# Nineteen relative features per head in a linear attention layer: the twentieth exponential as a preset one

## The chip, the cores and the metric

The kernel runs on one core of one Trainium2 chip. The metric is the device time of one execution in microseconds, the median over repeated runs; lower is better. The profiler records one execution and gives a span from the first to the last instruction of the program.

In the text PE is the tensor engine (matrix products), DVE the vector engine, ACT the scalar engine (activations), POOL the GpSimd engine, and SP the engine whose queue issues nearly all transfers.

## What is computed

A block with layernorm, a linear attention with softmax features, a residual, and a second layernorm with a SiLU feed-forward part and a residual. There are 2048 tokens of 640 values and 32 heads of 20.

```python
qkv = (layernorm(x) @ wqkv)              # q, k, v: 32 heads of 20
pq = einsum("bhsd,hdf->bhsf", q, w_phi)  # 20 features per head
pk = einsum("bhsd,hdf->bhsf", k, w_phi)
phi_q = concat([softmax(pq), softmax(-pq)])   # 40 per head
phi_k = concat([softmax(pk), softmax(-pk)])
kv = einsum("bhsf,bhsd->bhfd", phi_k, v)
z = phi_k.sum(over tokens)
o = einsum(phi_q, kv) / (einsum(phi_q, z) + 1e-6)
h = x + o @ wo
out = h + silu(layernorm(h) @ w1) @ w2        # w1: 640 x 1728
```

A softmax does not change when one number is subtracted from all its arguments. That is the fact which the change uses.

## The kernel before

The 2048 tokens are 16 tiles of 128, and the token index t runs over these. The program has these stages, which overlap:

- **Prologue.** PE is kept running with dummy products (`warm0` to `warm19`) while the key weights arrive in five pieces (`WK0` to `WK4`). Each piece is transposed (`wk`, evicted by `wke`), multiplied by the block diagonal of `w_phi` (`fk`, 640 columns in two banks) and evicted by ACT into `Wfk` (`fk0e` to `fk4e`). So the feature projection is folded into the key weights, and a key projection gives features at once. The same is done for the queries (`fq0` to `fq5`, into `Wfq`), from weights that a transposing transfer brings.
- **Normalisation** of a tile: `st` (moments, DVE), `rs` (inverse deviation, ACT or POOL), `xn` (the normalised tile, DVE or POOL), `xt` (its transpose, by PE for the first four tiles, by a transposing transfer on SP's queue for the others).
- **Keys and values**, per tile: `K` (ten matmuls of 320 columns), `ex` (two exponentials on ACT, of the features and of their negatives, into one of four key buffers `EK`), `su` (sums over each run of 20, DVE), `rk` (inverse of the sums, ACT), `sc` (scaling in place, DVE), `V` and `ve` (values, into one of eight buffers `VP`), `kv` (eleven matmuls that add the tile to the state of all heads). Each head has 40 features, each group of three heads one stationary operand of 128 columns.
- **Queries**, per tile: `Q` (ten matmuls; 33 heads' worth, one of them a head of zeros), `qe` (exponentials into `EQ`, all tiles in one buffer), `qs`, `ql`/`qi`/`qr` (sums, ratio, scaling of one half), `qt` (transpose by transfer).
- **Attention**, per tile: `D` (eleven matmuls), `E` (division, two halves), `ot` (transpose by transfer), `G` (output projection, two groups of five matmuls of 320 columns), `ga` (residual), `ls`, `lr`, `hn`, `ht` (second normalisation and its transpose).
- **Feed-forward**, for units of two or four tiles: `u` (up projection, up to 512 columns), `s` (SiLU), `d` (down projection), `oa` (residual), `out` (store).

The order of all these steps is written out by hand in one list, `ORDER`, of some 900 names. The program walks it and emits each step; each engine then runs its own instructions in that order and waits by semaphores. `su2` is the sum of tile 2, `G10` the first group of tile 1's output projection, `u0.12` the piece of unit 0 that begins at block 12. A dictionary `ON` says for some steps which engine they run on. The projections share three pairs of PSUM banks in turn (`ps_pair`), so a projection also waits until the one three places back has been evicted.

Of the kernel before, what the change touches and what calls it, by code (L numbers as in the profile page):

```python
# [18 lines left out]
warm0 warm1 warm2 warm3 warm4 warm5 warm6 warm7 warm8 warm9 warm10 warm11 warm12 warm13 warm14 pad0 mask  # L19
ones0 ones3 X0 st0 WK2 WK3 phi_a WK0 wk2 warm15 warm16 warm17 warm18 warm19 rs0 X1 phi_b WK1 WK4 wk3  # L20
wke2 wke3 wk0 wke0 xn0 xt0 X2 mask0 st1 wk1 wke1 fk3 wk4 x0 WV0 fk1 rs1 X4 fk3e fk1e fk2 xn1 own fk0 WV3
fk2e wke4 st2 V0.0 ones5 fk0e fk4 wph1 st3 xt1 K0s fk4e WV2 rs2 K0.2 x1 WV4 K0.1 st4 K0.0 xn2 K0.4 rs3
K0.3 ones1 ex0 K1 st6 V0.3 WV1 V0.2 rs4 su0 X8 xt2 V1 V0.1 ex1 xn3 xn4 x2 ve1 xt3 x3 wq2 V0.4 ve0 st5
rs5 K2 rk0 st9 st7 K3 wq3 su1 ex2 ex3 sc0 V2 ve2 wph0 rk1 st8 xn5 phq V3 xt4 rs9 st12 ve3 rs6 wq1 rs7
load10 kv0 ones2 xn6 K4 ex4 V4 sc1 fq3 ones7 ve4 rs8 kv1 xn7 xt5 wq0 xn8 xn9 fq3e xt6 V5 su2 xt7 wq5 rk2
su3 ve5 rk3 wq4 K5 sc2 ex5 fq0 K6 kv2 sc3 st11 kv3 fq0e xt8 fq2 ex6 st10 su4 fq2e su5 rs11 V6 ve6 st13
fq1 K7 st14 V7 fq1e rk4 xt9 rs10 xn10 ex7 zeros ve7 su6 rs13 V8 sc4 ve8 fq4 V9 ones4 load0 xt10 load5
fq5 fq4e rk5 rk6 su7 ve9 K8 sc5 xn11 kv4 load7 fq5e rs14 K9 rk7 sc6 rs12 ex8 kv5 Q0 sc7 ex9 qe0 xn14
ones6 K10 su8 xt11 xn12 kv6 load2 xn13 su9 st15 rs15 kv7 qs0 xt12 xn15 Q1 rk8 V10 ex10 sc8 qe1 ve10
load3 ql0 K11 V11 xt13 rk9 ex11 qs1 su10 qi0 ve11 ql1 eqp rk10 kv8 K12 V12 ex12 qi1 sc9 ve12 load4 su11  # L30
sc10 kv9 K13 rk11 V13 kv10 qr0 xt14 K14 su12 ex13 rk12 sc11 su13 ve13 xt15 ex14 rk13 K15 kv11 V14 Q2
ex15 qr1 qt0 load1 qt1 mask1 ve14 load6 V15 sc12 Q3 su14 kv12 su15 sc13 rk14 rk15 kv13 sc14 qe2 kv14
ve15 sc15 qs2 kv15 bd1 load9 qe3 Q5 Q7 halves ql2 qe5 qe7 bd0 qi2 qr2 qs3 D0 E00 E01 D1 E10 ql3 Q4 E11
qe4 qt2 Q9 qi3 Q6 qe9 qs5 ql5 D2 qi5 Q8 ot0 ot1 qr3 G00 G01 qs4 qe6 E20 qr5 E21 ql4 G10 ga01 Q10 qe8 qi4
ga00 qe10 ga10 qt3 Q11 D3 qr4 qt5 ls0 G11 qe11 Q14 Q12 E30 Q13 lr0 ot2 qe14 ga11 qe12 qe13 ls1 qt4 E31
hn0 lr1 ot3 Q15 G20 hn1 ht1 qs6 G21 qe15 qs7 ht0 D5 G30 load8 pad1 ga20 qr6 ga21 ga30 G31 load11 E50 E51
D4 u0.12 E40 u0.4 u0.0 s0.0 s0.12 ga31 ls3 u0.6 E41 ot5 qs8 u0.L u0.2 ls2 qr7 s0.6 u0.8 qt6 lr2 s0.4 ot4
u0.10 D6 s0.L G50 s0.10 G40 lt0 qt7 lr3 s0.8 E60 G51 E61 s0.2 d10 ot6 ga40 hn2 ga50 ga51 ls5 hn3 lr5 G41
d00 D7 d01 ga41 ls4 G60 lr4 hn5 G61 E70 ht2 ht3 hn4 oa10 ht5 d11 qr8 oa00 ht4 ga61 u2.2 u2.0 ga60 qt8
E71 ot7 s2.0 oa01 qs9 u2.L qs13 s2.2 qr9 oa11 qs11 u2.6 D8 u2.10 E80 ls6 qt9 u2.7 u2.3 s2.L u2.11 s2.10  # L40
s2.6 qr13 E81 u2.9 s2.9 qr11 u2.5 qs12 s2.7 qs10 s2.3 u2.1 D9 G70 s2.5 E90 qr10 u2.12 s2.11 E91 ot8 G71
u2.4 lr6 ga71 ga70 qt11 out0 lt2 s2.1 qt10 u2.8 out1 hn6 s2.4 qr12 ls7 G80 s2.8 ga80 ot9 G81 D11 s2.12
E110 d30 ht6 qt13 E111 d20 D10 ga81 lr7 G90 E100 oa30 oa20 E101 ot10 G91 hn7 ga91 d31 ot11 ga90 ls8 qs15
lr8 d21 qt12 oa31 d50 G100 ls9 G101 hn8 out3 d40 d51 ht8 lr9 hn9 oa21 ga101 G110 out2 ga100 ga110 oa50
oa40 G111 qs14 d41 oa51 D12 ls10 ht7 E120 ht9 u6.1 u6.0 oa41 ga111 u6.12 u6.8 D13 s6.0 s6.1 qr14 s6.8
E121 s6.12 u6.11 ot12 u6.2 u6.3 qr15 lr10 s6.11 u6.L s6.2 E130 ls11 out4 E131 u6.9 qt15 s6.3 G120 ot13
s6.L u6.6 lt6 s6.6 lr11 u6.7 u6.10 hn10 u6.5 out5 s6.7 hn11 s6.9 u6.4 qt14 G121 ga120 ga121 s6.5 ht11
G130 D14 G131 E140 ga131 s6.10 s6.4 d60 ls12 oa60 d61 d70 ht10 lr12 E141 d91 ga130 ls13 oa61 hn12 oa70
D15 lr13 d90 ht12 ot14 d71 hn13 ht13 out6 G140 oa71 oa90 u10.L oa91 ga140 out9 E150 u10.0 u10.1 out7
E151 u10.6 G141 u10.9 s10.L s10.0 s10.6 u10.8 ga141 d80 u10.7 s10.1 u10.3 u10.11 ot15 s10.3 u10.5 u10.12  # L50
oa80 s10.9 s10.8 s10.11 u10.2 u10.4 ls14 s10.7 s10.5 u10.10 s10.12 s10.4 G150 G151 lt10 lr14 d81 s10.10
s10.2 d110 hn14 oa81 ht14 out8 d111 ga150 d120 ga151 ls15 d101 lr15 d100 hn15 oa100 oa110 ht15 oa101
d121 oa111 out10 oa120 out11 u14.L u14.4 u14.0 oa121 s14.0 s14.L u14.8 u14.6 s14.6 u14.2 d131 u14.12
u14.10 s14.2 s14.4 d130 lt14 oa130 oa131 s14.12 s14.10 out13 s14.8 out12 d140 d141 oa140 d150 oa141
out14 d151 oa150 out150 d152 oa151 out151 oa152 out152
# [4 lines left out]
def kernel(  # L60
# [20 lines left out]
    DH = 20  # L81
    HF = 2 * DH
# [19 lines left out]
    proj_ctx = ctx.enter_context(ExitStack())  # L102
    proj = proj_ctx.enter_context(tc.tile_pool(name="proj", bufs=1, side="right"))
# [33 lines left out]
    NE = 4  # L137
# [56 lines left out]
    NV = 8  # L194
    VP = [persist.tile([P, H, HV], BF16, name=f"VP{i}") for i in range(NV)]

    EK = [persist.tile([P, FCH * (NCH - 1) + P], BF16, name=f"EK{i}") for i in range(NE)]
# [27 lines left out]
    Wfk = proj.tile([P, C, D], BF16, name="Wfk")  # L225
    Wfq = proj.tile([P, C, D + DH], BF16, name="Wfq")

    def ones(i):
        nc.gpsimd.memset(VP[i][:, :, DH:HV], 1.0)
        if i < NE:  # L230
            nc.gpsimd.memset(EK[i][:, H * HF :], 0.0)

# [17 lines left out]

    add("zeros", lambda: nc.gpsimd.memset(Wfq[:, 0, D : D + DH], 0.0))

# [70 lines left out]

    def folded(eng, Wf, key, ce):
        eng(Wf[:, ce, 0:D].rearrange("p (g n) -> p g n", g=2), ps_of.pop((key, ce))[:, :, 0:HD])  # L325
# [11 lines left out]
    LW = D - (NQ - 1) * QW  # L337
    WPQ = early.tile([P, NQ, DH], BF16, name="WPQ")
    own_q = early.tile([P, 2, BH], BF16, name="own_q")
    phi_q = early.tile([P, NQ, QW], BF16, name="phi_q")  # L340
# [49 lines left out]
    def width(r):  # L390
        return min(QW, D - QW * r)
# [13 lines left out]
    def folded_block(eng, r):  # L405
        eng(Wfq[:, :, QW * r : QW * r + width(r)], ps_of.pop(("fq", r)))
# [86 lines left out]
    def project(t, W, key):  # L493

        ps = ps_of[key, t] = ps_pair()
        for g in range(2):
            for c in range(C):
                nc.tensor.matmul(  # L498
                    ps[:, g, 0:HD],
                    XnT[:, c, t * P : (t + 1) * P],  # L500
                    W[:, c, g * HD : (g + 1) * HD],
# [19 lines left out]
    def first_key_chunk(c):  # L521

        first_keys.append(c)
        for g in range(2):
            nc.tensor.matmul(  # L525
                ps_of["K", 0][:, g, 0:HD], XnT[:, c, 0:P], Wfk[:, c, g * HD : (g + 1) * HD],
# [5 lines left out]
    def project_queries(t, g, ps):  # L532
        a, b = (DH * h for h in Q_PARTS[g])
        for c in range(C):
            e = b if c == 0 else min(b, D)
# [12 lines left out]
    def key_exps(t):  # L548
        ek[t] = EK[t % NE]
        p4 = ps_of.pop(("K", t))[:, :, 0:HD].rearrange("p g (h f) -> p g h f", f=DH)  # L550
# [416 lines left out]
```

## Time and profile before

| what | value |
|---|---|
| median of three runs | 234.9 us (234.73 to 234.98) |
| profiled execution, span | 232.8 us |
| granted clock of PE | 1.000 |
| busy, PE / DVE / ACT / POOL | 228.0 / 164.0 / 107.4 / 62.6 us |
| moved by DMA | 26.79 MB |

The span counts from the first to the last instruction of the program; the device time of a run holds what lies around it too. Of the profiled execution no other time is given than its span. In the rows of the profile a line such as "L498 PE MATMUL" is a group of instructions of one source line; the first numbers after the bar are its busy time in us and the mean of one in ns, the numbers behind the second bar are the idle time ahead of it and what ended it. In the chain of work that ended last and in the timeline, the first column is the start in us and the second the length; an "xN" is the number of instructions merged. A row of transfers ends with the median time from issue to landing.

### The profile page before, as it was taken

The page shows a single profiled execution, that of the slowest core. Times are in us where ns is not written, and L with a number is a line of the kernel's source. Part 1 is how long each engine was busy: PE and PEld are TensorE (multiplying, and loading weights), DVE is VectorE, ACT ScalarE, POOL GpSimd, SP SyncE. Part 2 cuts the span into 40 slices and gives each one's busy share as a digit, 9 for nine tenths or more (in the row PEclk, how much of TensorE's full clock was granted, in tenths as well). Part 3 has the DMA queues.
Part 4 walks back from the last instruction along what each step waited for, and adds up shares of the span by engine and source line. Part 5 has one row for each costly group of instructions (what it writes and reads, how often), then busy time and mean ns, then how long its engine had stood idle before and what let it go on. Part 6 is the DMA issues. An engine that isn't in the chain of part 4 may idle for free.

```text
span 232.8 us, 5040 instructions
## 1 busy us (share of the span) xinstructions
PE 228.0 (98%) x1977; PEld 160.5 (69%) x1984; DVE 164.0 (70%) x340; ACT 107.4 (46%) x241; POOL 62.6 (27%) x99
## 2 busy tenths in 40 slices
PE   7999999999999999999999999999999999999995
PEld 5777777777777778877545777655677455778874
DVE  4989999999999899998999794891472330404031
ACT  2899999998879884410344000064200235001400
POOL 7589896995001120211010111110020010100000
PEclk9999999999999999999999999999999999999999
DMA  6995379698836766696236956137213301011011
GB/s 169 336 291 103 87 119 217 217 145 188 220 115 114 159 116 136 124 121 146 56 66 154 120 114 158 30 80 172 55 28 85 99 0 28 31 28 56 8 56 56
DMA packets 67213, 26.79 MB, mean 115 GB/s; under 512 B 60151, under 2 KB 66167, under 8 KB 67063
## 3 DMA queue, kind: packets, MB, share of 16 engines
q1 hardware_dynamic: 66535, 26.47, 49.9%
q8 instruction: 15, 0.25, 0.5%
q10 hardware_dynamic: 656, 0.03, 0.2%
q14 instruction: 7, 0.06, 0.1%
HBM read 9.64 MB, written 2.62 MB: 53 GB/s over the span
## 4 chain that ended last, share of the span: by engine, by line
PE 95%; DMA 2%; SPq 1%; issue 1%; ACT 1%; DVE 0%
PE banks L890 24%; PE banks L850 24%; PE banks L498 18%; PE banks L536 9%; PE banks L767 9%; PE banks L589 2%; PE banks L734 2%; PE banks L893 2%; DMA Wk<-in_A_wqkv_dram 2%; PE banks L861 1%; PE banks L525 1%; PE banks L400 1%; ACT Wfk L325 1%; SPq L166 1%; PE banks L510 0%
## 5 line engine op out<-in xcount | busy, mean ns | idle before, releaser
L870 ACT ACTIVATE shT<-banks 128x512 bf16<-128x512 f32 (+1 forms) x53 | 28.5, 591 | 84.2 <-PE banks L850 84.2
L890 PE MATMUL banks<-w_sb,shT 128*128 128x320 bf16 (+2 forms) x429 | 61.3, 295 | 0.0
L850 PE MATMUL banks<-HnT,w_sb 128*128 128x512 bf16 (+1 forms) x318 | 58.4, 335 | 0.4
L890 PEld LDWEIGHTS <-shT 128*128 128x128 bf16 x429 | 41.1, 98 | 15.2
L850 PEld LDWEIGHTS <-w_sb 128*128 128x128 bf16 x325 | 31.2, 98 | 22.1
L899 DVE TENSOR_TENSOR o_t<-banks,X 128x320 bf16<-128x320 f32 (+2 forms) x33 | 14.9, 474 | 39.6 <-PE banks L893 26.7
L443 POOL TENSOR_SCALAR rs<-mv 128x1 f32<-128x1 f32 x21 | 5.8, 276 | 113.2 <-DVE mv L435 113.2
L498 PEld LDWEIGHTS <-XnT 128*128 128x128 bf16 x300 | 28.5, 98 | 10.3
L450 POOL TENSOR_SCALAR xn<-X,mv,rs 128x640 bf16<-128x640 bf16 x12 | 31.3, 2615 | 4.1 <-ACT rs L441 2.1
L434 DVE BATCH_NORM_STATS2 st<-X 128x6 f32<-128x320 bf16 x64 | 27.9, 477 | 4.3 <-DMA X<-in_A_x_dram 4.0
L767 PE MATMUL banks<-wo_sb,OT 128*128 128x320 bf16 x160 | 24.8, 299 | 0.0
L662 DVE TENSOR_REDUCE Sq<-EQ 128x66 f32<-128x1320 bf16 x16 | 23.9, 1512 | 0.0
L774 DVE TENSOR_TENSOR X<-banks,X 128x320 bf16<-128x320 f32 x32 | 14.7, 483 | 13.0 <-PE banks L767 12.9
L658 ACT ACTIVATE EQ<-banks 128x360 bf16<-128x360 f32 (+2 forms) x52 | 22.0, 514 | 3.2 <-PE banks L536 3.1
L557 DVE TENSOR_REDUCE Sk<-EK 128x64 f32<-128x1280 bf16 x16 | 23.3, 1468 | 0.2 <-ACT EK L553 0.2
L536 PE MATMUL banks<-Wfq,XnT 128*128 128x360 bf16 (+2 forms) x160 | 23.3, 299 | 0.0
L498 PE MATMUL banks<-Wv,XnT 128*128 128x320 bf16 x150 | 22.5, 299 | 0.0
L498 PE MATMUL banks<-Wfk,XnT 128*128 128x320 bf16 x150 | 22.5, 299 | 0.0
L553 ACT ACTIVATE EK<-banks 128x640 bf16<-128x640 f32 x32 | 20.5, 698 | 1.4 <-PE banks L498 1.2
L767 PEld LDWEIGHTS <-OT 128*128 128x128 bf16 x160 | 15.2, 98 | 6.5
L536 PEld LDWEIGHTS <-XnT 128*128 128x128 bf16 x160 | 15.2, 97 | 6.2
L747 DVE TENSOR_TENSOR O<-banks,Rd 128x360 bf16<-128x360 f32 (+1 forms) x32 | 15.7, 491 | 1.1
(76 smaller groups left out, 203.0 us busy)
## 6 DMA issues: line engine op xcount, KB each, us to landing
out_dram<-o_t SPq DMA_DIRECT2D x15, 160.0 KB, 2.0
w_sb<-in_B_w_dram SPq DMA_DIRECT2D x5, 432.0 KB, 4.8
w_sb<-in_B_w_dram SPq DMA_DIRECT2D x3, 480.0 KB, 4.1
X<-in_A_x_dram SPq DMA_DIRECT2D x1, 1280.0 KB, 8.4
Wk<-in_A_wqkv_dram SPq DMA_DIRECT2D x5, 160.0 KB, 3.8
Wv<-in_A_wqkv_dram SPq DMA_DIRECT2D x5, 160.0 KB, 4.9
wo_sb<-in_A_wo_dram SPq DMA_DIRECT2D x1, 800.0 KB, 6.5
X<-in_A_x_dram SPq DMA_DIRECT2D x1, 640.0 KB, 5.9
```

The lines of the kernel that those rows point to most:

```text
L434: nc.vector.bn_stats(st[:, i, :], X[:, t, i * HD : (i + 1) * HD])
L450: eng.tensor_scalar(out=xn_[t][:], in0=X[:, t, :], scalar1=mv_.pop(t)[:, 0:1], scalar2=rs_.pop(t)[:], op0=ALU.subtract, op1=ALU.mult,)
L498: nc.tensor.matmul(ps[:, g, 0:HD], XnT[:, c, t * P : (t + 1) * P], W[:, c, g * HD : (g + 1) * HD], start=(c == 0), stop=(c == C - 1),)
L536: nc.tensor.matmul(ps[:, 0 : e - a], XnT[:, c, t * P : (t + 1) * P], Wfq[:, c, a:e], start=(c == 0), stop=(c == C - 1),)
L553: nc.scalar.activation(E5[:, :, :, b, :], p4, AF.Exp, scale=sign)
L557: nc.vector.tensor_reduce(sk[t][:], ek[t][:, 0 : H * HF].rearrange("p (q f) -> p q f", f=DH), axis=AX.X, op=ALU.add)
L658: nc.scalar.activation(features(t, a, b)[:, :, :, i], p4, AF.Exp, scale=sign)
L662: nc.vector.tensor_reduce(sq[t][:], EQ[0][:, t, :, 0:FCH].rearrange("p c (q f) -> p c q f", f=DH), axis=AX.X, op=ALU.add)
L767: nc.tensor.matmul(ps[:, 0:HD], ot[t][:, c, :], wo_sb[:, c, g * HD : (g + 1) * HD], start=(c == 0), stop=(c == C - 1),)
L850: nc.tensor.matmul(ps[:, at : at + n], w1_sb[:, c, fc * P : fc * P + P], HnT[u][:, c, 0:n], start=(c == 0), stop=(c == C - 1),)
L870: nc.scalar.activation(shT[u][:, f0 * n : f1 * n], ps_of.pop(("u", u, f0))[:, 0 : (f1 - f0) * n], AF.Silu)
L890: nc.tensor.matmul(ps[:, 0 : b - a], shT[u][:, at : at + P], w2_sb[:, fc, a:b], start=(fc == 0), stop=False,)
```

## The change

Instead of 20 features per head the projections give 19: the folded matrix holds the columns of `w_phi` minus its last column. The twentieth feature is then always zero and its exponential always one. Its slot in the key buffers and in `EQ` is written by POOL: a memset of four-byte words, each two bfloat16 ones, covers slots 18 and 19 of each run, and the exponential then writes slots 0 to 18. As `sc` scales a key buffer in place, the slots are written again each time the buffer is used again (`ref5` to `ref15`, each after `kv` of the tile that used the buffer last); the first five are written within `ones0` to `ones4`, those of `EQ` by `eqr0` (tiles 0 to 3) and `eqr1`.

Key projections go from 320 to 304 columns a matmul. Query projections go from 660 and four times 640 columns a tile to 627 and four times 608. There are five key buffers for four and seven value buffers for eight; they move to a pool that is closed with the projection's tiles. The sums and scalings still run over 20 slots. The order of all steps is new.

```diff
+    DR = DH - 1
+    HR = H // 2 * DR
+    DP = H * DR
...
+    keys = proj_ctx.enter_context(tc.tile_pool(name="keys", bufs=1, side="right"))
...
-    NE = 4
+    NE = 5
...
-    NV = 8
-    VP = [persist.tile([P, H, HV], BF16, name=f"VP{i}") for i in range(NV)]
-    EK = [persist.tile([P, FCH * (NCH - 1) + P], BF16, name=f"EK{i}") for i in range(NE)]
+    NV = 7
+    VP = [keys.tile([P, H, HV], BF16, name=f"VP{i}") for i in range(NV)]
+    EK = [keys.tile([P, FCH * (NCH - 1) + P], BF16, name=f"EK{i}") for i in range(NE)]
...
-    Wfk = proj.tile([P, C, D], BF16, name="Wfk")
-    Wfq = proj.tile([P, C, D + DH], BF16, name="Wfq")
+    Wfk = proj.tile([P, C, DP], BF16, name="Wfk")
+    Wfq = proj.tile([P, C, DP + DR], BF16, name="Wfq")
+
+    TWO_ONES = 1.0 + 0x3F80 / 2**23
+
+    def reference_slots(i):
+        w = EK[i][:, 0 : H * HF].bitcast(F32).rearrange("p (q f) -> p q f", f=DH // 2)
+        nc.gpsimd.memset(w[:, :, DH // 2 - 1 : DH // 2], TWO_ONES)
 
     def ones(i):
         nc.gpsimd.memset(VP[i][:, :, DH:HV], 1.0)
         if i < NE:
             nc.gpsimd.memset(EK[i][:, H * HF :], 0.0)
+            reference_slots(i)
...
+    WPD = early.tile([P, C, DR], BF16, name="WPD")
...
+        if b == 0:
+            nc.vector.tensor_tensor(
+                WPD[:], WPH[:, :, 0:DR], WPH[:, :, DR:DH].to_broadcast([P, C, DR]), op=ALU.subtract
+            )
...
+    def eq_references(a, b):
+        w = EQ[0][:].rearrange("p t c f -> p (t c f)").bitcast(F32).rearrange("p (t c f) -> p (t c) f", c=NCH, f=P // 2)
+        r = w[:, a * NCH : b * NCH, 0 : FCH // 2].rearrange("p c (q f) -> p c q f", f=DH // 2)
+        nc.gpsimd.memset(r[:, :, :, DH // 2 - 1 : DH // 2], TWO_ONES)
+
+    add("eqr0", lambda: eq_references(0, 4))
+    add("eqr1", lambda: eq_references(4, T))
...
-        p4 = ps_of.pop(("K", t))[:, :, 0:HD].rearrange("p g (h f) -> p g h f", f=DH)
+        p4 = ps_of.pop(("K", t))[:, :, 0:HR].rearrange("p g (h f) -> p g h f", f=DR)
...
-            nc.scalar.activation(E5[:, :, :, b, :], p4, AF.Exp, scale=sign)
+            nc.scalar.activation(E5[:, :, :, b, 0:DR], p4, AF.Exp, scale=sign)
...
-            add(f"K{t}", lambda t=t: project(t, Wfk, "K"))
+            add(f"K{t}", lambda t=t: project(t, Wfk, "K", HR))
...
+        if t >= NE:
+            add(f"ref{t}", lambda t=t: reference_slots(t % NE))
```

The same replacement of 20 by 19 is made in the folds (two more subtractions on POOL within `phq`), in `project_queries` and in `query_exps`. Of the two orders, these are the stretches of which the text speaks; first the prologue, then the middle of the key stage, then the first output projections, then the first up projection:

```diff
-wke2 wke3 wk0 wke0 xn0 xt0 X2 mask0 st1 wk1 wke1 fk3 wk4 x0 WV0 fk1 rs1 X4 fk3e fk1e fk2 xn1 own fk0 WV3
+WK2 WK3 WK0 st0 warm15 wk2 warm16 own wk3 wke3 warm17 ones1 wk0 phi_b warm18 warm19 X1 rs0 WK1 pad0 wke2
+WK4 wke0 X2 st1 fk3 fk3e wk1 rs1 wk4 xn0 wke1 fk2 fk2e ones3 ones0 xt0 fk1 WV0 fk1e X4 wke4 mask xn1 fk0
...
-ones6 K10 su8 xt11 xn12 kv6 load2 xn13 su9 st15 rs15 kv7 qs0 xt12 xn15 Q1 rk8 V10 ex10 sc8 qe1 ve10
+xt11 rk6 kv5 K10 ex9 V11 rk7 xn12 su8 rk8 sc6 kv6 qe0 su9 ref10 xn14 ref11 xt12 rs15 ex10 sc7 Q1 K11
+xt14 rk9 ve11 xn13 V10 qe1 ex11 kv7 sc8 kv8 su10 K12 ve10 ref12 xn15 rk10 load4 eqr1 qs0 sc9 ex12 su11
...
-qe4 qt2 Q9 qi3 Q6 qe9 qs5 ql5 D2 qi5 Q8 ot0 ot1 qr3 G00 G01 qs4 qe6 E20 qr5 E21 ql4 G10 ga01 Q10 qe8 qi4
+Q7 halves bd0 D0 qe7 load11 qs3 qr2 qt2 E00 ql3 D1 E01 Q4 qe4 Q9 E10 ot0 qe9 Q6 E11 qi3 Q8 D2 qe6 qs5
+ot1 qs4 G01 E20 ql5 G10 qr3 G00 ga01 qe8 qt3 qi5 qr5 Q10 ga10 qt5 ga00 E21 ql4 G11 qi4 load6 qr4 Q11
...
-hn0 lr1 ot3 Q15 G20 hn1 ht1 qs6 G21 qe15 qs7 ht0 D5 G30 load8 pad1 ga20 qr6 ga21 ga30 G31 load11 E50 E51
-D4 u0.12 E40 u0.4 u0.0 s0.0 s0.12 ga31 ls3 u0.6 E41 ot5 qs8 u0.L u0.2 ls2 qr7 s0.6 u0.8 qt6 lr2 s0.4 ot4
+qe10 ga11 ls0 D3 Q14 Q12 qe11 ls1 Q15 E30 lr1 ot2 qe14 E31 Q13 qs6 qt4 qe12 D5 ot3 hn1 ht1 G20 lr0 hn0
+qr6 qe15 E50 qe13 E51 ga20 D4 G21 ht0 G31 qs7 G30 u0.L s0.L E40 qt6 ga21 E41 ga31 u0.6 qr7 u0.0 ga30 ls3
```

133 lines of the change are left out of this document (71 added, 62 removed).

## The prediction

> **What bounds the kernel now.** I read the page first, then the stages, then the chain.
>
> ```profile
> span 232.8 us, 5040 instructions
> ## 1 busy us (share of the span) xinstructions
> PE 228.0 (98%) x1977; PEld 160.5 (69%) x1984; DVE 164.0 (70%) x340; ACT 107.4 (46%) x241; POOL 62.6 (27%) x99
> ## 2 busy tenths in 40 slices
> PE   7999999999999999999999999999999999999995
> PEld 5777777777777778877545777655677455778874
> DVE  4989999999999899998999794891472330404031
> ```
>
> The tensor engine (PE) has no slice with a hole between the first and the last. The vector engine (DVE) is nearly as full up to the middle of the span. The profiled span is 232.8 us and the median of the runs 234.9, so 2.1 us lie around the span; I carry them over unchanged.
>
> ```profile
> 0.00:10.40 10.40, 8.85 (x86) 6.76 (x87) 6.96 (x18) 5.23 (x9) 6.63 (x28) 1.00 0.80 240
> 10.40:65.30 54.90, 54.74 (x534) 40.97 (x531) 52.75 (x79) 51.35 (x120) 40.85 (x34) 1.00 0.78 185
> 65.30:91.00 25.70, 25.70 (x277) 19.37 (x275) 24.08 (x50) 19.60 (x55) 3.69 (x9) 1.00 0.57 107
> ```
>
> These are the stages by window (length; then busy PE, weight loads, DVE, ACT, POOL; clock; DMA): prologue, keys and values, queries. In the key stage PE stands still for 0.16 us of 54.9, DVE for 2.15, ACT for 3.55. So each matmul column removed is worth its time only if DVE and ACT bring their results earlier too. DVE is the second bound, 2 us behind the first.
>
> **Columns.** The chain has stretches in which PE waits for nothing:
>
> ```profile
> 46.64 4.07 PE banks L498 x30
> ...
> 159.20 5.40 PE banks L850 x25
> ```
>
> L498 is 320 columns: 4.07/30 = 135.7 ns. L850 is 512: 5.40/25 = 216.0 ns. The difference, 80.3 ns over 192 columns, is 0.418 ns a column. Keys: 16 tiles x 10 matmuls x 16 columns fewer = 2560 columns, 1.07 us. Queries: 660 + 4 x 640 becomes 627 + 4 x 608, 161 columns fewer a tile, 2576 in all, 1.08 us. Query folds: 25 matmuls by 6 and 5 by 2 columns, 160, 0.07 us. **Sum 2.22 us.** The key folds lose 230 columns (0.10 us), but in the prologue, which has another limit, below.
>
> Wfq's rows become 627 elements long, so half the moving operands of the queries start at an odd element. The nearest row of the chain is L589, whose operand starts at 63c:
>
> ```profile
> 65.67 1.35 PE banks L589 x44
> ```
>
> There half of the starts are odd too, and the mean is 1.35/44 = 30.7 ns where 63 columns at 0.418 take 26.3. So an odd start costs between nothing and some 8 ns; since L589 also takes a new weight per matmul, I take nothing. At 8 ns on half of 160 query matmuls it would be 0.6 us.
>
> The Trainium skill speaks against the sum here: "TensorE: Matmul & The Clock Gate", section "Back-to-back issue gap", has a sustained 81 ns at 128 columns and 131 ns at 512, since weight loads and matmuls are paced together. That would be 0.13 ns a column and a saving of 0.7 us in place of 2.22 (an estimate from that page). The trace's 216.0 ns at 512 columns disagrees, and the measurement decides.
>
> **Prologue.**
>
> ```profile
> 9.44 1.30 ACT Wfk L325 x2
> ...
> 10.78 1.52 PE banks L525 x10
> ```
>
> The first key matmul waits for five folded pieces that ACT evicts one after the other, and in the chain that stands behind the landing of the last weight rows. The new order puts fold fk3 and its eviction ahead of the last two weight transposes. That can gain at most one eviction (1.30/2 = 0.65 us), at least nothing, since the four others still follow the landing. I take 0.25. The floor is then 234.9 - 2.22 - 0.25 = **232.4**.
>
> **Other engines' work.**
>
> ```profile
> L553 ACT ACTIVATE EK<-banks 128x640 bf16<-128x640 f32 x32 | 20.5, 698 | 1.4 <-PE banks L498 1.2
> ...
> L418 POOL MEMSET EQ<- 128x1408 bf16 x1 | 1.3, 1270 | 0.0
> ...
> L231 POOL MEMSET EK<- 128x48 bf16 x4 | 0.8, 228 | 0.0
> ```
>
> ACT's key exponentials shrink by between nothing and 5% of 20.5 us (1.0 us). That keeps ACT level with PE; it is no gain of its own. DVE's sums and scalings still cover all 20 slots: nothing goes. DVE gains one subtraction of 95 elements a partition at the very start. The nearest row is the 280 elements of L747 below, 0.45 us; I take 0.3. POOL gains the memsets. From 228 ns for 48 elements and 1270 for 1408, 0.77 ns an element, one of 64 words takes 0.24 us and the 264 words of eqr0 0.39. Whether 4-byte words at a stride are dearer no row shows; twice that is my upper end. 16 memsets per key buffer use are some 4 us, all on POOL, which is not the bound. But ref{t} waits for keys_values(t-5), and what stands behind it in POOL's queue, the next normalisation, waits too; the next key exponentials wait for the memset.
>
> Three edits I cost at nothing. Seven value buffers for eight make values(t) wait for keys_values(t-7); in the new order at least four projections lie on PE between the two, and if that cover went, ACT would stand for one of them, 1.36 us. The late tiles lie over the key buffers now, whose last reader, kv15, is on PE ahead of every D; the first silu comes after the last query. The end is as it was: d152, one addition, one store, so what follows PE's last matmul stays.
>
> **What is late next.** Where the new order has the same PE steps ahead of a step as the old one, PE comes to it earlier by exactly the columns saved; the producer comes earlier only by what it stood idle. Three places are tight.
>
> First, G10, the output projection of tile 1:
>
> ```profile
> 17.09 0.89 DVE L434 BATCH_NORM_STATS2 st<-X 128x6 f32<-128x320 bf16 x2 [0.89 <-DMA X<-in_A_x_dram]
> ```
> ```profile
> 67.13 0.46 DVE L598 TENSOR_TENSOR KVB<-banks,mask 128x294 bf16<-128x294 f32 x1 [0.42 <-PE banks L589]
> ```
> ```profile
> 72.65 0.45 DVE L747 TENSOR_TENSOR O<-banks,Rd 128x280 bf16<-128x280 f32 x1
> ```
> ```profile
> 73.85 1.23 SPq L758 DMA_TRANSPOSE OT<-O  x1
> ```
> ```profile
> 76.08 2.20 PE L767 MATMUL banks<-wo_sb,OT 128*128 128x320 bf16 x15
> ```
> ```profile
> OT<-O SPq DMA_TRANSPOSE x16, 2.6
> ```
>
> Before, O of tile 1 is done at 73.10, its transpose lands at 73.85 + 2.6 = 76.45, and PE reaches its first projection at 76.08 and G10 two groups later. After, the same set of steps (16 K, Q0 to Q9, all fq) is ahead of the first projection: 1.07 + 0.67 + 0.07 + 0.25 = 2.06 earlier, 74.02, and G10 follows after one group, 5 x 135.7 ns = 0.68, at 74.70. DVE's steps ahead of E11 are the same set. They can win back the 0.89 us wait for X (the first step that reads tiles 8 and up now stands behind one more step, st7) and the 0.42 us wait for kv15, less 0.3: 1.0. The transpose then lands near 75.4, 0.7 us after PE wants it; if nothing is won back, at 76.75, 2.05 late.
>
> Second, the first up projection, u0:
>
> ```profile
> 84.62 0.69 DVE L450 TENSOR_SCALAR xn<-X,mv,rs 128x640 bf16<-128x640 bf16 x1
> ```
> ```profile
> 86.83 2.00 SPq L794 DMA_TRANSPOSE HnT<-xn  x1
> ```
> ```profile
> 90.74 1.47 PE L850 MATMUL banks<-HnT,w_sb 128*128 128x256 bf16 x12
> ```
> ```profile
> HnT<-xn SPq DMA_TRANSPOSE x16, 2.4
> ```
> ```profile
> L662 DVE TENSOR_REDUCE Sq<-EQ 128x66 f32<-128x1320 bf16 x16 | 23.9, 1512 | 0.0
> ```
>
> PE comes 2.22 + 0.25 earlier, at 88.27. DVE has one more sum (qs6, 1.5) ahead of the second hn, 85.31 + 1.5 + 0.3, less up to 1.3 of waits won back (0.89 and 0.42): 85.8 to 87.1. With 2.4 for the transpose it lands at 88.2 to 89.5, or 0.7 later where SP is late with it, as it was before (84.62 + 0.69 to 86.83): 0 to 1.9 us late.
>
> Third, K13:
>
> ```profile
> 40.11 3.14 POOL L450 TENSOR_SCALAR xn<-X,mv,rs 128x640 bf16<-128x640 bf16 x1 [2.08 <-ACT rs L441]
> ...
> 43.30 4.98 POOL L450 TENSOR_SCALAR xn<-X,mv,rs 128x640 bf16<-128x640 bf16 x2
> 48.26 0.89 POOL L443 TENSOR_SCALAR rs<-mv 128x1 f32<-128x1 f32 x1
> 49.23 0.57 POOL L446 TENSOR_TENSOR rs<-rs,nhalf_t 128x1 f32<-128x1 f32 x1
> ```
> ```profile
> 53.95 1.52 PE L498 MATMUL banks<-Wfk,XnT 128*128 128x320 bf16 x10
> ```
> ```profile
> XnT<-xn SPq DMA_TRANSPOSE x12, 3.3
> ```
>
> xn13, the second of the pair at 43.30, ends at 48.28 and lands near 51.6; K13 starts at 53.95, after the change at 53.95 - 0.25 - (13 + 2) x 0.067 - 0.07 = 52.63. Ahead of xn13 now stand seven memsets (1.7), eqr0 (0.4), rs15 (1.4) and two small subtractions (0.6), less one memset; against them the wait of 2.08, which the later place of xn14 removes. Net 0.8 (if short POOL instructions overlap) to 1.8: landing at 52.4 to 53.4, 0 to 0.8 late; 2.9 late if the wait stays.
>
> A slip of PE at one place gives every later one more time, so the largest counts, not the sum. I take 0.8, between 0.3 and 1.6: 232.4 + 0.8 = **233.2** (232.7 to 234.0).
>
> **Rivals.** *All of it arrives.* DVE and POOL win back their waits in full and PE meets no gap: 232.4. For it: they are idle for 2 us in the key stage for reasons that the new order moves. Against: all three places above are tight. Chance 0.22. *DVE gives it back.* DVE wins back nothing, PE waits 2.05 us for O at G10: 232.4 + 2.05 = 234.5, up to 235.4 with a further wait at u0. For it: DVE's work does not shrink by one instruction. Against: the 0.89 and 0.42 us above are idle. Chance 0.15. *POOL makes it slower.* The memsets take their places in POOL's queue and wait there for keys_values; xn13 behind them is late by the 2.08 not won back, by 1.8 of work and by a further 1.0 of holding: K13 waits 3.9 us, 232.4 + 3.9 = 236.3. It turns the sign once xn13 ends after some 52.3 us, 4 us later than now. For it: POOL is busy 40.85 of 54.9 us there. Against: it is 26% idle. Chance 0.20. *The change doesn't do what it says*: weight loads, not columns, pace PE, and the streams get no cheaper: 234.9 - 0.25 = 234.65. Against: weight loads are busy 40.97 us of 54.9, and 512 columns take 80 ns more than 320. Chance 0.02. (The page named above lies between: 234.9 - 0.7 - 0.25 = 233.95, an estimate from its figures.)
>
> **How the numbers follow.** My forecast has 0.41. The border of faster and slower is 0.2% (0.47 us), about what a measurement of this kernel can tell from no change. Faster: 0.41 + 0.22 + 0.03 of the give-back = 0.66. Same: 0.10 of the give-back and 0.02 = 0.12. Slower: 0.20 + 0.02 = 0.22. The range runs from a little under the floor, 232.0 (a prologue gain of the full 0.65), to 236.0, which leaves out the worst half of the POOL case.
>
> **What would show it.** K and Q groups of ten at 1.29 us in place of 1.36; key and query matmuls together 2.1 us less. First key matmul at 10.5 or before. DVE's 0.89 us wait near 17 us gone. PE idle after the first key of 0.3 to 1.6 us, at G10 or u0, put down to OT or HnT. If PE's idle time exceeds 2.9 us, or it stands at K13, the POOL case was right; if L536 keeps 136 ns a matmul, the odd starts cost.

## Result, and the profile after

| kernel | median | runs, lowest to highest | ratio to before, 95% interval |
|---|---|---|---|
| before | 234.94 us | 10, 234.62 to 236.03 | |
| after | 237.64 us | 10, 235.88 to 237.83 | 1.0097 [1.0075, 1.0120] |

The change makes the kernel 1% slower, 2.7 us. The forecast was 233.2 us (232.0 to 236.0), and slower had 0.22. The profiled execution of after took 237.82 us with a span of 235.9, 3.1 us more than before's 232.8.

The page of after, first and second part:

```profile
span 235.9 us, 5087 instructions
## 1 busy us (share of the span) xinstructions
PE 226.9 (96%) x1975; PEld 159.9 (68%) x1984; DVE 164.6 (70%) x341; ACT 106.7 (45%) x241; POOL 65.4 (28%) x119
## 2 busy tenths in 40 slices
PE   7899999899999997999999999999999999999995
```

PE is busy for 1.1 us less and the span is longer: behind the prologue PE now has two slices with a hole, the eighth (41 to 47 us) and the sixteenth (88 to 94 us). Before it had none. The stages of after, by the same windows (length; then busy PE, weight loads, DVE, ACT, POOL; clock; DMA):

```profile
0.00:10.40 10.40, 7.94 (x77) 5.83 (x78) 6.65 (x16) 4.97 (x9) 6.62 (x35) 1.00 0.81 254
10.40:65.30 54.90, 53.24 (x542) 40.76 (x541) 51.99 (x80) 49.76 (x117) 45.13 (x48) 1.00 0.73 169
65.30:91.00 25.70, 25.29 (x267) 18.95 (x265) 24.60 (x52) 21.50 (x59) 2.81 (x8) 1.00 0.89 149
91.00:160.00 69.00, 67.52 (x571) 46.03 (x574) 61.37 (x147) 14.06 (x27) 7.08 (x19) 1.00 0.63 109
```

PE is now idle for 1.66 us of the key stage (before 0.16), 0.41 of the query stage (0.00) and 1.48 of the stage behind it (0.26). In the key stage DVE and ACT are idle for more than before too (2.9 and 5.1 us for 2.2 and 3.6): no engine has become the bound, they wait for each other. DMA is busy for 0.89 of the query stage for 0.57 before. What PE waited for (us in total, times, longest):

```profile
PE banks L534 <- DMA XnT<-xn: 1.6, 2, 1.1
PE banks L899 <- DMA HnT<-xn: 1.1, 1, 1.1
PE banks L313 <- DMA Wk<-in_A_wqkv_dram: 0.9, 1, 0.9
PE banks L493 <- DVE xn L486: 0.4, 1, 0.4
PE banks L772 <- DMA EqT<-EQ: 0.3, 1, 0.3
```

L534 is the key and value projection (L498 before), L899 the piece u0.L with which the first up projection now begins, L772 the attention product. Behind the prologue all of them wait for transposing transfers.

The list of waits leaves out what is short. So I also use PE's **lateness**: the start of a step minus the summed column time of all PE steps ahead of it, in the order of that kernel. It stays constant while PE runs without gaps, and rises at each gap. All in us, from the traces:

| kernel | first key matmul | Q8, ahead of the output projections | first up projection | D8 | end |
|---|---|---|---|---|---|
| before | 4.37 | 4.39 | 4.38 | 4.34 | 4.22 |
| after | 4.83 | 7.06 | 9.25 | 9.23 | 9.57 |

Before loses nothing after its first key matmul. After is 5.35 us later at the end (9.57 less 4.22); the columns give 2.3 back, and the difference is the 3.1 us of the spans.

### The profile page after: what moved, and what is told of

Same layout as the page of the kernel before. It is cut to its first block, busy times and chain, and to the rows that moved or that the text cites. A ratio compares the mean times of both kernels' runs of the same rounds, so it can differ in the third digit from the quotient of the medians.

```text
span 235.9 us, 5087 instructions
## 1 busy us (share of the span) xinstructions
PE 226.9 (96%) x1975; PEld 159.9 (68%) x1984; DVE 164.6 (70%) x341; ACT 106.7 (45%) x241; POOL 65.4 (28%) x119
## 4 chain that ended last, share of the span: by engine, by line
PE 70%; DVE 12%; DMA 9%; ACT 3%; issue 2%; POOL 1%; DVEq 0%; POOLq 0%; ACTq 0%
PE banks L888 23%; PE banks L928 22%; PE banks L534 8%; PE banks L805 7%; PE banks L572 4%; DMA XnT<-xn 3%; DVE st L470 3%; DMA OT<-O 2%; PE banks L931 2%; DMA EqT<-EQ 2%; DMA HnT<-xn 2%; PE banks L772 1%; DVE Sq L700 1%; DMA WPH<-in_A_w_phi_dram 1%; DVE Sk L593 1%
## 5 line engine op out<-in xcount | busy, mean ns | idle before, releaser
L908 ACT ACTIVATE shT<-banks 128x512 bf16<-128x512 f32 (+1 forms) x53 | 29.0, 588 | 63.7 <-PE banks L888 63.6
L534 PEld LDWEIGHTS <-XnT 128*128 128x128 bf16 x300 | 28.4, 98 | 11.5 <-DMA XnT<-xn 1.9
L479 POOL TENSOR_SCALAR rs<-mv 128x1 f32<-128x1 f32 x21 | 4.7, 226 | 105.9 <-DVE mv L471 105.9
L486 POOL TENSOR_SCALAR xn<-X,mv,rs 128x640 bf16<-128x640 bf16 x12 | 32.5, 2710 | 0.8 <-ACT rs L477 0.5
L696 ACT ACTIVATE EQ<-banks 128x342 bf16<-128x342 f32 (+2 forms) x52 | 21.5, 518 | 4.2 <-PE banks L572 4.1
L534 PE MATMUL banks<-Wfk,XnT 128*128 128x304 bf16 x150 | 21.3, 293 | 1.6 <-DMA XnT<-xn 1.6
L534 PE MATMUL banks<-Wv,XnT 128*128 128x320 bf16 x150 | 22.5, 299 | 0.1
L572 PE MATMUL banks<-Wfq,XnT 128*128 128x342 bf16 (+2 forms) x160 | 22.3, 293 | 0.0
L589 ACT ACTIVATE EK<-banks 128x608 bf16<-128x608 f32 x32 | 20.2, 694 | 2.5 <-PE banks L534 2.4
```

Source lines behind the costliest of these rows:

```text
L486: eng.tensor_scalar(out=xn_[t][:], in0=X[:, t, :], scalar1=mv_.pop(t)[:, 0:1], scalar2=rs_.pop(t)[:], op0=ALU.subtract, op1=ALU.mult,)
L534: nc.tensor.matmul(ps[:, g, 0:w], XnT[:, c, t * P : (t + 1) * P], W[:, c, g * w : (g + 1) * w], start=(c == 0), stop=(c == C - 1),)
L572: nc.tensor.matmul(ps[:, 0 : e - a], XnT[:, c, t * P : (t + 1) * P], Wfq[:, c, a:e], start=(c == 0), stop=(c == C - 1),)
L589: nc.scalar.activation(E5[:, :, :, b, 0:DR], p4, AF.Exp, scale=sign)
L696: nc.scalar.activation(features(t, a, b)[:, :, :, i, 0:DR], p4, AF.Exp, scale=sign)
L908: nc.scalar.activation(shT[u][:, f0 * n : f1 * n], ps_of.pop(("u", u, f0))[:, 0 : (f1 - f0) * n], AF.Silu)
```

## Which half of the change loses

Two runs separate the two halves: the features with the old order, and the new order without the features. Both keep the five key and seven value buffers. In the first, `ones4` therefore comes earlier and `ones7` goes, and `eqp` moves by a few steps.

```diff
# a_old_order_19: after, with the order of before; the new steps put in:
+ref5, ref6 behind xn7; ref7, ref8 ahead of rs10; eqr0, ref9 behind fq5e; ref10 behind xn14;
+ref11 ahead of xn13; ref12 ahead of xn15; ref13 to ref15 behind kv8 to kv10; eqr1 behind mask1
# b_new_order_20: after's order, 20 features, no ref or eqr steps; five key and seven value buffers stay
-    DR = DH - 1
+    DR = DH
```

> The 19 features with everything that belongs to them (memsets, two subtractions, five key buffers, seven value buffers), but in the order of before; each ref{t} stands on POOL behind kv{t-5}, where POOL was idle or between two normalisations. If the loss lies in the new order, PE saves its 2.2 us of columns and meets few gaps: 232.4 to 233.4 us. If it lies in the features (memsets in POOL's queue, exponentials that wait for them), it stays at 236 us or more.

> The new order with 20 features: 320 columns a key matmul again, no memsets of ones, no subtractions; five key and seven value buffers stay. If the loss lies in the order, its gaps stay and PE gets 2.2 us of columns back, part of which fills gaps: 237.5 to 239.8 us. If it lies in the features, 235.5 us or less.

Measured: 233.46 us (ratio 0.9946 [0.9913, 0.9978]) and 238.01 us (1.0144 [1.0117, 1.0171]). So **the features save time and the new order loses more than they save**. The new order with 20 features has its gaps at the same places (lateness 4.69, 6.70, 8.24, 8.22, 8.76 in the columns above).

The execution that was profiled of the first had one late transfer (PE waited 2.25 us for Wv in the prologue), so I ran it again.

> The old order with 19 features and presets once more, for a trace of an execution without the late Wv load. Theory (the features save 1.5 of their 2.2 us here because only the slip at the first attention products is left): 233.0 to 233.8, first key matmul near 10.5, one gap of 0.3 to 1 at the first output products near 75 us. Rival (each stage slips a little in the old order too): several gaps, sum over 1 us.

Measured: 233.36 us (233.22 to 234.32), ratio 0.9924 [0.9902, 0.9946], span 231.3. PE's waits after the start of the program:

```profile
PE banks L493 <- DVE xn L486: 0.4, 1, 0.4
PE banks L313 <- DMA Wk<-in_A_wqkv_dram: 0.3, 1, 0.3
PE banks L534 <- DMA XnT<-xn: 0.2, 1, 0.2
PE banks L625 <- DVE EK L606: 0.2, 1, 0.2
```

The first two lie in the prologue. Lateness: 4.23, 5.14, 5.17, 5.14, 5.02. The first key matmul starts at 10.55 us. The 0.8 us over before come from two short waits (kv0 for DVE's scaling at 21.76, K6 for its transpose at 28.73); 2.3 less 0.8 is the span's 1.5. The theory had the place wrong (there is no gap at the output projections) and the sum right.

## Where the new order loses it

```diff
# h1_old_keys_new_rest: the steps ahead of "halves" in the old order, the rest in the new one
# h2_new_keys_old_rest: the reverse
```

> 19 features and presets throughout; the steps up to the halves stand in the old order, the rest in the new one. Theory (each stage of the new order loses its own): the key stage has no slip, the later ones (0.4 at the first attention products, 0.5 before the dense layer, 1.3 at the first up-projection, 0.45 after) stay, some 2.6 us on top of the 233.46 of the old order with 19 features: 235.5 to 236.3. Rival (the loss is the key stage's alone): 233.2 to 233.8.

> 19 features and presets throughout; the new order up to the halves, the old one for the rest. Theory (each stage of the new order loses its own): the slips at xt6 and xt10 and of the first stage stay (0.46 + 0.2 + 0.6 + 1.3 = 2.6 us), the later ones go: 235 to 236. Rival (the later stage alone loses): 233.2 to 233.8.

Measured: 236.64 us (1.0065 [1.0045, 1.0086]) and 235.63 us (1.0022 [1.0001, 1.0042]). Against 233.36 the late half costs 3.3 us and the key half 2.3; together they would be 5.6, and after has lost 4.3. Each half loses its own, and the sum overstates them by 1.3. The waits of h1 and of h2:

```profile
PE banks L899 <- DMA HnT<-xn: 0.9, 1, 0.9
...
PE banks L772 <- DMA EqT<-EQ: 0.7, 1, 0.7
PE banks L805 <- DMA OT<-O: 0.6, 1, 0.6
```
```profile
PE banks L533 <- ACT Rk L601: 1.1, 1, 1.1
...
PE banks L533 <- DMA XnT<-xn: 0.5, 1, 0.5
```

(h2's 1.1 us is put down to ACT; it is K10 at 45.27 us, and in the trace the transpose of tile 10 landed at 45.22.) Lateness of h1 is 4.21, 4.67, 6.90, 6.88, 7.67; of h2 5.32, 7.53, 7.75, 7.71, 7.59.

**The key half.** Up to the landing of tile 10's normalised rows, the chain of after runs through GpSimd (first column start, second length):

```profile
31.48 1.65 POOL xn L486
...
33.50 0.57 POOL rs L482
...
37.85 6.91 DMA XnT<-xn
...
44.80 2.82 PE banks L534 x20
```

The transpose of tile 10 takes 6.91 us; before it took 5.21, since there one load was ahead of it on SP's queue, and here there are four, as SP's timeline shows:

```profile
34.41 0.59 SPq L526 DMA_DIRECT2D w_last<-in_B_w_dram  x1
35.04 0.58 SPq L526 DMA_DIRECT2D w_sb<-in_B_w_dram  x1
35.66 0.51 SPq L526 DMA_DIRECT2D wo_sb<-in_A_wo_dram  x1
36.21 0.52 SPq L526 DMA_DIRECT2D w_sb<-in_B_w_dram  x1
37.85 3.87 SPq L515 DMA_TRANSPOSE XnT<-xn  x2
```

And the normalisation ahead of it takes 3.65 us on POOL where others take 2.5. Two scalings of DVE lie beside it (timelines of POOL and DVE of after):

```profile
34.17 3.65 POOL L486 TENSOR_SCALAR xn<-X,mv,rs 128x640 bf16<-128x640 bf16 x1
...
37.90 2.50 POOL L486 TENSOR_SCALAR xn<-X,mv,rs 128x640 bf16<-128x640 bf16 x1
```
```profile
33.96 1.55 DVE L606 TENSOR_TENSOR EK<-EK,Rk 128x1280 bf16<-128x1280 bf16 x2
```

Before, no scaling lay beside xn10, and it took 2.52.

First I moved the loads alone, in two ways, and took the presets away in a third kernel.

```diff
# c_loads_back: load0, load2, load9, load10 to behind xt11, xt12, xt13, xt13
-xt9 ... load10 load9 ... load0 ... load2 K9 fq5e xt10 Q0 sc5 eqr0 xt11
+xt9 ... K9 fq5e xt10 Q0 sc5 eqr0 xt11 load0
# l_all_loads: all twelve weight loads and wq4, wq5 at their old places among the transposes
# d2_no_refs: after without the steps ref5 to ref15
-            add(f"ref{t}", lambda t=t: reference_slots(t % NE))
```

> The kernel after, with four weight loads moved on SP's queue from ahead of xt10 to behind xt11, xt12 and xt13. If those loads (1.8 MB with w1 and wo) hold up the transpose of tile 10, its landing falls from 6.9 us after issue to 4 or less, PE's 1.1 us gap at K10 goes and the time falls to 236.0 to 236.8 us, less if nothing downstream asks for it again. If POOL is what is late there, 237.3 to 237.8 us.

> The changed kernel, with the twelve MLP weight loads and the loads of Wq's last two parts back at their old places among the transposes; compute steps stay in the new order. Theory (loads issued ahead of a transpose hold it back on SP's queue): the gaps at K6, K10, G01, D4 and u0 shrink, 4.3 us of them at most, the first stage's 0.46 stays: 234.2 to 236.0. Rival (the order of the work on VectorE and GpSimd is late, not the queue): 237.0 to 237.8, gaps as before.

> The changed kernel without the steps ref5 to ref15, so 44 of the short presets are left out and the twentieth exponential of later uses of a buffer isn't preset (their sums are not the reference's). Theory (the presets lie beside other work of GpSimd): 237.2 to 237.8. Rival (they make GpSimd late for the transposes' inputs): GpSimd is done earlier with xn10, the gap at K10 goes, 236.5 or less.

Measured: c 237.55 us (four runs, 235.72 to 239.06: too few and too wide to tell it from after), l 237.98 (237.67 to 238.67), d2 237.27 (236.70 to 239.63). The presets are hidden: d2 (which leaves out eleven of them, not the 44 of its expectation) stays within the expected interval, and its gap at K10 is still there (1.3 us). Moving the loads gave nothing back by itself. In c tile 10's transpose took 2.57 us and K10's gap went, and a gap of 0.80 us came at K15. That one c made itself: load9 and load10 stand ahead of tile 15's transpose there, which took 5.20 us for 2.80 in after. In l the transpose took 3.45, and the gap came at V11, ten matmuls later (l's waits):

```profile
PE banks L899 <- DMA HnT<-xn: 1.2, 2, 1.0
PE banks L534 <- DMA XnT<-xn: 1.2, 1, 1.2
```

Tile 11 is normalised behind tile 10 on POOL (37.92 to 40.42 us in l, 35.53 to 38.03 before), and the new order of PE asks for it early: V11 stands right behind K10, where before Q1 and V10 lay between K10 and the first use of tile 11. So there are three causes in a row: the queue, the scalings and PE's own order. The next two runs take out the second and then the third.

```diff
# l2_loads_scales: l_all_loads, and sc3 behind rk3, sc4 behind rk4
-ex6 rk3 ... rk4 K7 su5 V7 rs10 fq1e ex7 sc3 ... V8 sc4 ones6 xn10
+ex6 rk3 sc3 ... rk4 sc4 K7 su5 V7 rs10 fq1e ex7 ... V8 ones6 xn10
# m1_values_swapped: l2, and V10, ve10 change places with V11, ve11
```

> The changed kernel with the loads at their old places (as l_all_loads), and the scales sc3 and sc4 issued as soon as their factors are there, so that they don't lie beside xn10 on GpSimd. Theory (the two scales stop xn10 for 1.15 us, and that is what is left of the key stage's gap): xn10 takes 2.5 instead of 3.65, xn11 ends 1.1 earlier, the 1.2 us gap at V11 shrinks to 0.3 or less: 236.7 to 237.2. Rival (GpSimd is late from before): xn11's end moves less than 0.5, gap 0.8 or more, 237.6 to 238.

> As l2_loads_scales, with the value projections of tiles 10 and 11 in each other's places, so that PE first needs tile 11's transpose 2.5 us later. Theory (the new order of PE's steps asks for xt11 before GpSimd can have it): the 0.83 us gap ahead of V11 goes. If the closed gap is kept, 236.0 to 236.3; if it is handed to the places behind, as in l4_three_parts, the waits for OT, HnT or EqT between 75 and 96 us grow by as much and the time stays at 236.6 to 237.1. I expect the second (0.6 to 0.4).

Measured: l2 236.89 us (1.0067 [1.0041, 1.0093]), m1 237.37 (1.0105 [1.0080, 1.0129]). xn10 took 3.18 us in l2, as sc4 still lay beside it; one scaling costs POOL 0.7 us, two 1.15. V11's gap shrank from 1.2 to 0.8 us, and l2's time fell by 1.1 against l, as expected. The gap gave only 0.4 of it, so the agreement is in part luck: in the profiled executions l2 also came to its first key matmul 0.9 us before l (10.29 us for 11.17), with the same order of steps up to there. In m1 the gap at V11 was gone, and the time was no better (it is above both expectations; in the profiled execution 0.45 us of it were lost in the prologue already). In both a new gap stood at D6, for tile 6's queries (l2's waits, then m1's):

```profile
PE banks L772 <- DMA EqT<-EQ: 1.3, 1, 1.3
PE banks L534 <- DMA XnT<-xn: 0.8, 1, 0.8
```
```profile
PE banks L772 <- DMA EqT<-EQ: 1.0, 1, 1.0
```

This gap was of my making. SP's timeline of l2 has load8 and load11, at their old places, ahead of that transpose:

```profile
89.28 0.58 SPq L526 DMA_DIRECT2D w_sb<-in_B_w_dram  x1
89.91 0.51 SPq L526 DMA_DIRECT2D w_last<-in_B_w_dram  x1
90.58 2.31 SPq L742 DMA_TRANSPOSE EqT<-EQ  x1
```

The old order can have them there, since it asks for D6 later.

**The late half.** In after, the second layernorm waits behind a sum (DVE's timeline: O of tile 3, qs6, then hn1 and hn0):

```profile
84.91 0.45 DVE L785 TENSOR_TENSOR O<-banks,Rd 128x280 bf16<-128x280 f32 x1
85.28 1.52 DVE L700 TENSOR_REDUCE Sq<-EQ 128x66 f32<-128x1320 bf16 x1
86.71 0.80 DVE L486 TENSOR_SCALAR xn<-X,mv,rs 128x640 bf16<-128x640 bf16 x2
```

```diff
# q_h1_sum_later: h1_old_keys_new_rest, and
-E31 Q13 qs6 qt4 qe12 D5 ot3 hn1 ht1 G20 lr0 hn0 qr6
+E31 Q13 qt4 qe12 D5 ot3 hn1 ht1 G20 lr0 hn0 qs6 qr6
```

> Old order up to the halves, new order after, as in h1_old_keys_new_rest, but the sum qs6 stands behind hn0 instead of ahead of hn1. Theory (qs6's 1.5 us on VectorE make both HnT inputs late): hn1 is done 1.5 us earlier, the 0.9 us gap ahead of the first up-projection goes to 0.2 or less, the time falls by 0.7 to 0.9 against h1: 235.7 to 235.9. Rival (SP's queue, which stands behind ot3, sets HnT): gap 0.6 or more, 236.3 or more.

Measured: 236.14 us (235.03 to 236.80), between the two expectations by the time, and the 0.9 us gap at the first up projection is not in its trace any more. The waits for OT (0.8) and EqT (0.6) are.

**All of them at once.** l4 joined the loads, the scalings, qs6 and the old prologue; n1 joined these with the swap of m1, and put load8 and load11 back to where the new order has them.

```diff
# l4_three_parts: l2, qs6 behind hn0, the steps ahead of K0s in the old order (st0 ahead of phi_a)
# n1_conflicts_out: m1, the same two edits, and
-ht0 load8 load11 ... qt6
+qt0 load8 load1 ... qt1 load11 load6 load9 ... ht0 ... qt6
```

> As l2_loads_scales, with qs6 behind hn0, and the steps that precede the first key matmul in the old order (st0 ahead of the difference of phi). Theory (the losses are these four places): prologue 0.5, key stage 1.2, first up-projection 1.0 less than l_all_loads' 238.0: 235.0 to 235.8. Rival (each gap that is closed is handed to the next): 236.5 or more.

> As m1_values_swapped, with the steps ahead of the first key matmul in the old order, qs6 behind hn0, and the loads load8 and load11 where the new order has them (in l2, l4 and m1 they stood ahead of qt6 on SP's queue, and PE waited 1.0 to 1.3 us for qt6 at D6). Theory (the loss is a set of single conflicts, and each one that is taken out without a new one stays won): no gap over 0.3 us after the first key matmul, 234.3 to 235.3. Rival (the new order hands every closed gap to the next place): one or two gaps of 0.5 us or more again, 236.2 to 237.4.

Measured: l4 237.20 us (1.0097 [1.0064, 1.0130]), so the rival's side; n1 **234.30** us (0.9975 [0.9950, 1.0001]), the theory's lower end, though one gap is over its 0.3 us (V0.3 waits 0.55 us for Wv at 12.5 us). l4 still had the conflict at D6 (0.9 us) and a fold waiting 0.7 us for its weights, and its prologue won nothing over l2's (first key matmul at 10.72 us for 10.29). n1's waits after the start of the program, and its key stage by windows:

```profile
PE banks L546 <- DMA Wv<-in_A_wqkv_dram: 0.5, 1, 0.5
PE banks L493 <- DVE xn L486: 0.4, 1, 0.4
PE banks L899 <- DMA HnT<-xn: 0.3, 1, 0.3
PE banks L805 <- DMA OT<-O: 0.2, 1, 0.2
```
```profile
10.40:65.30 54.90, 54.11 (x544) 41.36 (x544) 52.05 (x79) 50.36 (x120) 45.20 (x53) 1.00 0.73 173
```

Lateness 4.19, 5.26, 5.73, 5.70, 6.34. Of the 4.3 us that separate after from the old order with the features, n1 wins back 3.3, and behind the first key matmul its order of PE's steps is after's but for V10 and V11. So most of the loss is a set of single conflicts, in which a transfer, a scaling or a sum stands ahead of the one that PE needs next. They have to be taken out together: the kernels with some of them left (l, l2, m1, l4) lie between 236.9 and 238.0. What the last 0.9 us are, I did not follow further; the wait for Wv is one part in the profiled execution.

**The best version.** The old order with the features has a gap left at K6. I tried to close that one.

```diff
# n2_old_wq0_later: a2_old_order_19, and
-wq0 xn8 xn9 fq3e xt6
+xn8 xn9 fq3e xt6 wq0
# and fq0, fq0e change places with fq1, fq1e
```

> The old order with 19 features and presets; the load wq0 stands behind the transpose xt6 instead of ahead of it, and the folds fq0 and fq1 change places so that fq0 finds its weights. Theory (the 0.2 us gap at K6 is xt6 behind wq0): the gap goes, xt6 takes 2.6 instead of 4.4 us, 232.9 to 233.2. Rival (xt6 is slow for another reason, or fq0 now waits): 233.3 or more.

Measured: 233.23 us (232.98 to 233.74), ratio 0.9914 [0.9883, 0.9945], not to be told from 233.36. The theory fell: with nothing ahead of it tile 6's transpose still took 4.70 us (4.38 in a2) and the gap was 0.5 us. In l2, m1 and n1, where it was issued at 23.3 to 23.6 us instead of 24.3, it took 2.6; in h1, issued at 23.4, it took 4.25. What else may hold it stands in the last section. Both versions beat before and after; a2 is the simpler one.

## Why the prediction was wrong, by its steps

- **Columns: right.** The groups of ten take 1.30 us, as forecast (chain of after, a stretch without a wait):

```profile
52.60 1.30 PE banks L534 x10
```

  By groups, key projections went from 22.5 to 21.3 us and queries from 23.3 to 22.3, 2.2 us in all. This is the groups view, before and then after:

```profile
L498 PE MATMUL banks<-Wfk,XnT 128*128 128x320 bf16 x150 | 22.5, 299 | 0.0
...
L536 PE MATMUL banks<-Wfq,XnT 128*128 128x360 bf16 (+2 forms) x160 | 23.3, 299 | 0.0
```
```profile
L534 PE MATMUL banks<-Wfk,XnT 128*128 128x304 bf16 x150 | 21.3, 293 | 1.6 <-DMA XnT<-xn 1.6
...
L572 PE MATMUL banks<-Wfq,XnT 128*128 128x342 bf16 (+2 forms) x160 | 22.3, 293 | 0.0
```

  Odd starts cost nothing that shows. The 0.7 us that I had estimated from the Trainium skill, "TensorE: Matmul & The Clock Gate", section "Back-to-back issue gap", is not borne out: 2.2 us were measured.
- **Prologue: wrong in sign in the profiled execution.** Forecast was a gain of 0.25 us; the first key matmul came at 11.15 us instead of 10.78. I looked at the folds and not at DVE's first step. `phi_a` now stands ahead of `st0` and holds the new subtraction, which waits for `w_phi` (chain of after):

```profile
0.78 2.76 DMA WPH<-in_A_w_phi_dram
3.57 0.27 DVE WPD L297
```

  So st0 started at 4.49 us for 3.12, and xn0, which the second half of the prologue hangs on, ended at 8.62 for 6.51. The late st0 alone does not cost the time. In l2, with the same order up to there, st0 is as late (4.55), but xn0 takes 0.39 us where it takes 1.29 in after, and the first key matmul comes at 10.29, earlier than in any other trace. xn0 takes 0.39 in c, d2, l2 and m1, where the memsets of `ones3` on POOL begin 0.12 to 0.13 us after it, and 1.18 to 1.57 in after, l and h2, where they begin 0.09 after it or before it. So the new place of these memsets is the likely cause, and hundredths of a us decide whether they lengthen xn0; no run moves them alone. (c, d2 and m1 lose time to late key weights instead, in one wait of 0.26 to 0.72 us for the last piece, and start at 10.74 to 11.83.)

  With the old order the first key matmul came at 10.54 and 10.55 (h1, a2), 0.24 before 10.78. That it is near my 0.25 is luck: fold fk3 stands at its old place there, and what is shorter is ACT's five evictions (2.92 us for 3.24, with 608 columns for 640). The gain that I meant shows in l2 alone, 0.26 us ahead of a2 (one execution of each).
- **G10: right.** I had PE 0.7 us ahead of OT. In h1, the kernel where PE comes there without the slips of the key stage, its lateness rises by 0.15 at G01 and 0.60 at G10. In after only 0.4 is left of it, at G01; PE was late by then. DVE's 0.89 us wait near 17 us was gone, as forecast.
- **u0: right.** Forecast 0 to 1.9 us late because of qs6; 1.1 measured, and q_h1 shows that qs6 is the cause. In after PE and the transpose both come there some 4 us later than I had put them, so h1's 0.9 us is the better test.
- **K13: wrong place.** No gap there. POOL's wait of 2.08 us went, as I had hoped, and the short presets cost what I had said (mean 239 ns for 240; eqr0 more, 0.61 us for 0.39) without effect on the time. The key stage stood at K6 (0.47 us) and K10 (1.12).
- **What I had not priced: the loads and the scalings.** The prediction sought the places where PE's inputs are tight by counting DVE's and POOL's work. I did not go through SP's queue, in which four loads had moved ahead of tile 10's transpose, and did not ask which DVE steps now lie beside which normalisation on POOL. Both are visible in the two orders.
- **"The largest counts, not the sum": the step that failed most.** I took 0.8 us for all the places behind the first key matmul; 4.9 were lost there. The slips were 0.46 us (prologue), 0.2 (V5), 0.6 (K6), 1.3 (K10), 0.4 (G01), 0.5 (D4), 1.3 (u0) and 0.3 to 0.5 behind it; with shorter ones they come to 5.35. The rule holds only where the later input doesn't come from PE itself. Here it does: O comes from D, the second layernorm from G, and EqT from Q. DVE's waits of after show how a slip is passed on:

```profile
DVE Sk L593 <- ACT EK L589: 2.0, 3, 1.0
```

  Three times in the key stage DVE waited for exponentials, which ACT makes from PE's key projections. Before, such waits came to 0.2 us, and n1, with the new order and few gaps, has none (it waits 1.4 us in the key stage for inverses of the sums instead). So DVE, the second bound, was late too: its first division came at 71.77 us, 1.22 later than before, although D0 did not hold it there (a sum and a scaling of its own stood right ahead). In n1, where PE lost less, it came at 69.96. The next place is then nearly as tight as it was. Not all of a slip is passed on: the two halves lose 5.6 us one by one and 4.3 together.
- **The rivals.** "POOL makes it slower" had the sign and, by its 236.3, half of the loss, but through a wait at K13 that didn't come. "DVE gives it back" describes h1's half (the late places G10 and u0 behind DVE), but I gave it 235.4 at most, and h1 took 236.64. That the features in the old order take 233.36 us, near the 233.2 that was forecast for the whole change, is luck: the 0.8 us of the forecast were for G10 and u0 in the new order, and the 0.8 us of a2 are lost at kv0 and K6.

## What to carry to other kernels

When an order written by hand is replaced, go through each queue on its own, the transfer queue first: list for each transpose which loads are now issued ahead of it, and for each step that PE needs next what stands ahead of it on its engine. Slips add up, for the most part, where the stages feed each other in a loop; the largest alone can count only where the later input is independent of the engine that slipped. And measure a change with two halves as two kernels before any finer experiment; it took one run each to see that one half was worth 0.5% (0.8% when run again) and the other cost 1.4%.

## What was not expected of the hardware

- A scaling on DVE with two inputs (0.77 to 0.82 us) and a normalisation on POOL (2.5 us) that begin close to each other lengthen one of the two, and a few hundredths of a us decide which. Where the scaling began up to 0.46 us ahead, or no more than 0.11 behind, the normalisation took longer: 3.65 us beside two scalings in after, 3.19 beside one in n1 (begun 0.11 behind it), 2.73 beside one begun 0.46 ahead in after. Where the scaling began 0.17 us behind (a2) it was the scaling, 1.37 us, and 0.96 where it began 0.59 behind (h1); the normalisation kept its 2.5. Where it began 0.96 us behind (l2), neither was longer. The Trainium skill says in "SBUF — State Buffer", section "Who interferes with whom", that a DVE instruction with two SBUF inputs contends with a GpSimd instruction that reads SBUF. The Trainium skill also calls the shared ports an exclusive lock, and says that issue order decides who blocks. The trace agrees that order decides, but for the 0.11 us. It shows no lock for the whole normalisation: a2's scaling ended at 29.09 us, 0.95 before the normalisation did.
- A transpose behind large loads is slow for as long as these take. Tile 10's took 6.91 us behind four loads in after and landed at 44.76, 0.75 after the last of them. Behind one load it took 5.21 before (issued 1.9 us after the load) and 3.45 in l (issued 3.4 after it), and landed 0.62 and 0.75 us after the load both times. With no load in flight, in c, it took 2.57. The landing of the transposes of xn, EQ and O in after was 2.6 to 3.8 us by group on the median, so one such place is worth more than a microsecond.
- Tile 6's transpose took 4.2 to 4.7 us in before, after, h1, h2, l, c, a2 and n2, 5.7 in l4 and 2.6 in l2, m1 and n1, with or without a weight transfer ahead of it, and not by the time of its issue alone (23.4 us in h1, 23.6 in m1). The packets in the traces show what goes with it: at 25.2 to 26.8 us every one of these kernels has a transfer of the kind "instruction", one packet of 16 KB that takes 1.0 to 1.4 us (queue q8 of the DMA view). In l2, m1 and n1 the transpose has sent its last packet by then. In the others it is still under way. In h1 its last two packets, of 4 bytes, come at 26.56 us, where the instruction packet ends at 26.57, and before at 26.97 for 26.99; the landing follows 1.1 us later. That the instruction transfer holds it is not tested by a run.
